# Attention scores from three half-height products, two heads at once on the row halves of TensorE, in place of two full-height products a head

## The chip, the cores and the metric

The kernel runs on one core of one Trainium2 chip. TensorE (PE) multiplies, VectorE (DVE), ScalarE (ACT) and GpSimd (POOL) work element by element, SyncE (SP) issues transfers. The metric is the device time of one execution in microseconds; of several runs the median counts.

## What is computed

Talking-heads attention over 4 batches of 12 heads with 448 positions of 64 channels, then a dense layer pair with a softmax-weighted activation:

```python
scores = scale * np.matmul(q, k.transpose(0, 1, 3, 2))
scores = np.einsum('bhij,hg->bgij', scores, w_pre)      # mix of the 12 heads
attn = softmax over j
attn = np.einsum('bhij,hg->bgij', attn, w_post)
x = np.matmul(attn, v)                                  # 1792 tokens x 768
h = x @ w_in;  solu = h * softmax(h);  layer norm * g_ln;  out = ln @ w_out
```

## The kernel before

Each float32 operand of the scores is split into two float16 parts, hi and lo, so that q times k is hi·hi + hi·lo + lo·hi. The tile `hl` holds, for every head, chunk and channel, hi and lo side by side: 2 x 64 channels make 128 columns, so a transpose of 112 x 128 puts hi on one half of the 128 rows and lo on the other. `turn_in` (L411) has SP issue these transposes as DMAs into `k1` and `q2`; for k of the first batch `turn_pe` (L427) transposes on PE and `turn_out` copies. In `q2` the halves lie the other way round than in `k1`, so that one product over 128 rows gives hi·lo + lo·hi. For hi·hi there is a second copy of q, `q1`, whose other half is zero: `clear_q1` (L455) sets the three tiles of it to zero once on POOL, and `move_hi` (L458) copies the hi half over by DMA after each transpose, one issue for a pair of heads, from ACT's queue in the first batch and from SP's afterwards.

`qk` (L473) makes the scores of one head and one block: two products of 448 columns, `q2` then `q1`, into one bank of `ps_s`, of which there are two. A batch is cut into four blocks of 88 or 120 rows (`ROWS`, L138). `score_hi` (L482) on ACT and `score_lo` (L488) on DVE empty the bank into the hi and lo part of the tile `s`; the bank is free after `score_lo`. In the first block of all, every other head uses a bank of `ps_o` (`spare`, L469).

Then the work goes in units of 10 rows, 45 in a batch. `fetch` (L506) has SP gather the rows of all 12 heads from `s` into `sr`, `premix` (L511) mixes heads with three products into `pm`, `rowmax`, `expo`, `guard`, `invert` and `weigh` (DVE, ACT, POOL) make the softmax, `postmix` (L557) mixes heads again (`po`), `post_out` empties it on ACT, and once a block is full `av` (L594) multiplies with v into `px`: 48 products that alternate between the two column halves of the array. `s` has two buffers, so the scores of a block are made while the block before it is consumed. After the last batch (from about 480 us) follow the dense layers, which the change does not touch.

The order of all instructions on all engines is made by the class `Plan` (L19): a list scheduler that simulates the engines with a cost in us for each task (`add`, L773 on), a due time, and rings (`ring`, `until`) for buffers: a task of ring `s` can only be placed when the holder two before it is done. Each engine executes its instructions in that order. `add_tasks` (L773) holds the tasks; those of the scores stand at L913 to L941, those of the transposes and the copy at L862 to L881.

Of the kernel before, what the change touches and what calls it, by code (L numbers as in the profile page):

```python
# [18 lines left out]
class Plan:  # L19
# [7 lines left out]
    def __init__(self, **rings):  # L27
        self.size = rings
        self.tasks = {}

    def add(self, key, run, on, after=(), behind=(), due=0.0, ring=None, until=(), lat=0.0):

        self.tasks[key] = (run, on, list(after), due, ring, list(until), lat, list(behind))

    def order(self):
# [10 lines left out]
        def ready(k, e):  # L46
# [5 lines left out]
            if ring and len(held[ring]) >= self.size[ring]:  # L52
                for a in held[ring][-self.size[ring]]:
# [6 lines left out]
        while len(out) < len(tasks):  # L60
# [27 lines left out]
            if ring:  # L88
                held[ring].append(until)
# [10 lines left out]
def kernel(  # L100
# [41 lines left out]
    QCH = 120  # L142
# [248 lines left out]
    def pair_views(n, b, p):  # L391
        x = raws[n, b][:, 2 * p : 2 * p + 2].rearrange("p h (c d) -> p (h c) d", c=NCH)
        y = hls[n, b][:, 2 * p : 2 * p + 2].rearrange("p h c s d -> p (h c) s d")
        i = (p + (n == "q")) % 2
        return x, y[:, :, i], y[:, :, 1 - i], scl[n, b][0][0:CP]

    def pair_hi(n, b, p, eng):
        if p == 0:
            hls[n, b] = hl_p.tile([CP, H, NCH, 2, D], F16, tag="hl", name=f"hl_{n}{b}")
# [3 lines left out]
    def pair_lo(n, b, p, eng):  # L403
# [4 lines left out]
        else:  # L408
            split_lo(lo, x, s, hi)

    def turn_in(n, b, p, m):  # L411
# [4 lines left out]
        if p == 0:  # L416
            x[b, g] = qk_p.tile([128, 2 * GP, S], F16, tag=f"{n}_{g}", name=f"{n}_{b}_{g}")
        h = 2 * GP * g + 2 * p
        nc.sync.dma_start_transpose(
            out=x[b, g][:, 2 * p : 2 * (p + m)].rearrange("p e (c i) -> p (e c) i", c=NCH),  # L420
            in_=hls[n, b][:, h : h + 2 * m].rearrange("p h c s d -> p (h c s d)"),
# [5 lines left out]
    def turn_pe(p):  # L427
        ps = tps[p] = ps_m.tile([128, 2, S], F16, tag="m", name=f"pt_{p}")
        for e in range(2):
            for c in range(NCH):  # L430
                nc.tensor.transpose(
                    out=ps[:, e, c * CP : (c + 1) * CP],
                    in_=hls["k", 0][:, 2 * p + e, c].rearrange("p s d -> p (s d)"),
# [3 lines left out]
    def turn_out(p, eng):  # L437
        g, i = divmod(p, GP)
        if i == 0:
            k1[0, g] = qk_p.tile([128, 2 * GP, S], F16, tag=f"k_{g}", name=f"k_0_{g}")  # L440
        copy(eng, k1[0, g][:, 2 * i : 2 * i + 2], tps.pop(p))
# [3 lines left out]
    def warm(e):  # L445
# [3 lines left out]
        x = hls["k", 0][:, 0, :, 0].rearrange("p c d -> p c d")  # L449
# [19 lines left out]
    def spare(b, c, h):  # L469

        return b == 0 and c == 0 and h % 2
# [34 lines left out]
    def fetch(b, u):  # L506
        c, r, step, _ = unit_rows(b, u)
        d = sr[b, u] = sr_p.tile([UK, 2, S], F16, tag="sr", name=f"sr_{b}_{u}")
# [896 lines left out]
```

## Time and profile before

| | us |
|---|---|
| median of 3 runs | 733.37 |
| lowest and highest run | 726.63, 737.01 |
| span of the profiled execution | 726.0 |
| PE busy, share of the span | 659.8, 91% |
| DVE, ACT, POOL busy | 495.6, 449.7, 275.4 |

The profile is of one execution; its span is that of the engines' instructions. Products are pipelined, so the durations shown for two products in a row overlap; the distance of their starts is what a product costs when PE is full. "Idle before" is the time in which an engine had nothing to run ahead of a group, with the work that ended it.

### The profile page before, as it was taken

To read this page: it belongs to the slowest core of one execution; us is meant where nothing else is said; L and a number is where in the kernel's file an instruction comes from. 1 tells how busy PE (TensorE), PEld (TensorE's weight loads), DVE (VectorE), ACT (ScalarE), POOL (GpSimd) and SP (SyncE) were. 2 spreads that over 40 slices of the span, in tenths; PEclk is the share of its full clock that TensorE was granted. 3 is DMA by queue.
4 is the path that set the end of the run, shared out by engine and by line. 5 is a ranking of instruction groups with operands and counts; after the bars stand their busy time and mean duration, and the time that the engine had idled before them with its cause. 6 is when DMAs were issued, how large, how long until landed. Compare 5 with 4: busy or idle time off the path is not lost.

```text
span 726.0 us, 14785 instructions
## 1 busy us (share of the span) xinstructions
PE 659.8 (91%) x5206; PEld 479.6 (66%) x5206; DVE 495.6 (68%) x1482; ACT 449.7 (62%) x956; POOL 275.4 (38%) x384
## 2 busy tenths in 40 slices
PE   3487998999997999999999989999998848999998
PEld 2346887888886878877888878774443424566664
DVE  6777996688985778996779999848888764200000
ACT  2567787787786787788788778744555544321111
POOL 6404781134851124771113353603667622320000
PEclk9789999999999999999999999999999989999999
DMA  8736497247577347677256645536456312243112
GB/s 228 121 90 199 136 221 212 84 135 228 180 198 200 87 105 213 199 209 212 95 180 204 212 153 188 139 98 187 121 121 151 68 20 51 51 103 95 44 44 65
DMA packets 121473, 102.47 MB, mean 141 GB/s; under 512 B 75524, under 2 KB 112056, under 8 KB 121400
## 3 DMA queue, kind: packets, MB, share of 16 engines
q1 hardware_dynamic: 115128, 87.07, 43.0%
q0 software_dynamic: 4384, 12.40, 6.4%
q10 hardware_dynamic: 1888, 2.07, 1.0%
q8 instruction: 41, 0.67, 0.4%
q14 instruction: 32, 0.26, 0.1%
HBM read 33.24 MB, written 9.63 MB: 59 GB/s over the span
## 4 chain that ended last, share of the span: by engine, by line
PE 61%; DVE 14%; DMA 11%; POOL 5%; ACT 3%; issue 2%; SPq 2%; DVEq 0%; POOLq 0%; ACTq 0%
PE po L561 15%; PE y L1314 14%; PE pm L515 12%; PE ps L480 9%; PE px L601 8%; DMA sr<-s 7%; PE ps_h L764 3%; DVE cv_wo L699 2%; POOL wo L702 2%; DVE cv_wo L694 1%; DMA raw_q<-in_q_dram 1%; DVE u L1257 1%; DVE wi L222 1%; DVE wo_l L222 1%; DMA q<-q 1%
## 5 line engine op out<-in xcount | busy, mean ns | idle before, releaser
L561 PEld LDWEIGHTS po<-wr,e 120*112 120x112 f32 x1440 | 173.5, 177 | 19.0 <-POOL wr L553 6.3
L561 PE MATMUL po<-wr,e 120*112 120x120 f32 x1440 | 178.6, 267 | 2.9 <-POOL wr L553 2.8
L553 POOL TENSOR_SCALAR wr<-wq,sm 120x120 f32<-120x120 f32 x180 | 78.0, 434 | 257.6 <-DVE sm L549 117.3
L532 ACT ACTIVATE e<-pm,nb,c_exp 120x448 f32<-120x448 f32 x180 | 131.4, 731 | 15.0 <-DVE e L520 9.5
L520 DVE TENSOR_SCALAR_CACHE_REDUCE e<-pm,c_nexp 120x448 f32<-120x448 f32 x180 | 121.2, 676 | 22.2 <-PE pm L515 12.5
L491 DVE SCALAR_TENSOR_TENSOR s<-ps,s 120x448 f16<-120x448 f32 (+1 forms) x192 | 116.9, 618 | 20.3 <-ACT s L486 17.9
L226 ACT COPY p_t<-po 112x480 f32<-112x480 f32 x180 | 104.0, 578 | 32.8 <-PE po L561 31.3
L486 ACT ACTIVATE s<-ps 120x448 f16<-120x448 f32 (+1 forms) x192 | 104.0, 548 | 28.1 <-PE ps L480 20.7
L515 PE MATMUL pm<-sr,wp_hi 120*120 120x448 f16 x360 | 100.5, 361 | 17.9 <-DMA sr<-s 16.8
L480 PE MATMUL ps<-k,q 128*120 128x448 f16 (+1 forms) x384 | 107.4, 366 | 7.8 <-DVE s L491 3.5
L764 PE MATMUL ps_h<-wi,xf 128*128 128x512 f16 x396 | 87.5, 379 | 3.7 <-DVE u L1257 3.6
L1314 PE MATMUL y<-wo_h,lth 128*128 128x384 f16 (+2 forms) x224 | 72.7, 331 | 9.9 <-ACT wo_h L217 9.9
L601 PE MATMUL px<-p_t,raw_v 112*64 112x120 f32 (+1 forms) x1536 | 80.7, 261 | 0.0
L601 PEld LDWEIGHTS px<-p_t,raw_v 112*64 112x64 f32 x1536 | 73.8, 137 | 8.7 <-issue 3.1
L1314 PE MATMUL y<-wo_l,lth 128*128 128x384 f16 (+2 forms) x224 | 72.7, 331 | 2.5 <-DVE wo_l L222 2.0
L1314 PEld LDWEIGHTS <-lth 128*128 128x128 f16 x448 | 44.3, 99 | 43.9 <-issue 15.3
L1314 PE MATMUL y<-wo_h,ltl 128*128 128x384 f16 (+2 forms) x224 | 72.8, 331 | 0.0
L764 PEld LDWEIGHTS <-xf 128*128 128x128 f16 x396 | 38.5, 98 | 49.2 <-issue 4.5
L515 PEld LDWEIGHTS <-wp_hi 120*120 120x120 f16 x360 | 43.2, 134 | 34.4 <-DMA sr<-s 19.9
L480 PEld LDWEIGHTS <-q 128*120 128x120 f16 (+1 forms) x384 | 47.8, 134 | 26.7 <-issue 10.4
L515 PE MATMUL pm<-sr,wp_lo 120*120 120x448 f16 x180 | 64.1, 356 | 0.0
L1322 ACT ACTIVATE o<-y,c_out 128x384 f32<-128x384 f32 (+2 forms) x28 | 16.1, 578 | 72.4 <-PE y L1314 72.4
(168 smaller groups left out, 820.6 us busy)
## 6 DMA issues: line engine op xcount, KB each, us to landing
sr<-s SPq DMA_DIRECT2D x180, 210.0 KB
cv_wi<-in_moe_w_in_dram SPq DMA_DIRECT2D x24, 256.0 KB
cv_wo<-in_moe_w_out_dram SPq DMA_DIRECT2D x8, 768.0 KB
raw_k<-in_k_dram POOLq DMA_DIRECT2D x18, 224.0 KB, 4.4
raw_q<-in_q_dram POOLq DMA_DIRECT2D x18, 224.0 KB, 4.2
raw_v<-in_v_dram POOLq DMA_DIRECT2D x18, 224.0 KB, 3.6
q<-q SPq DMA_DIRECT2D x18, 112.0 KB
xh<-xsh SPq DMA_DIRECT2D x9, 224.0 KB
```

The lines of the kernel that those rows point to most:

```text
L226: nc.scalar.copy(out=out, in_=in_)
L480: nc.tensor.matmul(y, x[:, e, i0 : i0 + n], k1[b, g][:, e], start=(a == 0), stop=(a == 1))
L486: nc.scalar.activation(out=s_t[b, c][0 : y.shape[0], h, 0], in_=y, func=AF.Copy, scale=2.0**-E_S)
L491: nc.vector.scalar_tensor_tensor(out=t[:, h, 1], in0=y, scalar=2.0**-E_S, in1=t[:, h, 0], op0=ALU.mult, op1=ALU.subtract)
L515: nc.tensor.matmul(ps[:, 0:S], w[0:UK], x[:, z], start=(a == 0), stop=(a == 2))
L520: nc.vector.tensor_scalar(out=e, in0=pmx[b, u][:, 0:S], scalar1=c_nexp[0:UK, b : b + 1], scalar2=None, op0=ALU.mult, op1=ALU.min, accum_ou ...
L532: nc.scalar.activation(out=ee[b, u], in_=pmx.pop((b, u))[:, 0:S], func=AF.Exp, bias=nbs.pop((b, u)), scale=c_exp[0:UK, b : b + 1], accum_o ...
L553: ENG[eng].tensor_scalar(out=w, in0=wq[0:UK, 0 : H * UN], scalar1=sums.pop((b, u)), scalar2=1.0, op0=ALU.mult, op1=ALU.mult)
L561: nc.tensor.matmul(ps[:, c * 120 : (c + 1) * 120], e[:, c * CP : (c + 1) * CP], w, start=True, stop=True)
L601: nc.tensor.matmul(xps[b, blk, g][e * 64 : e * 64 + 64, i, 0:n], raws["v", b][:, h, c * D : (c + 1) * D], block_view(b, blk, c * H + h), s ...
L764: nc.tensor.matmul(ps[:, n], xx[:, kc, o : o + 128], ww[:, kc, n * 512 : (n + 1) * 512], start=(kc == 0 and a == 0), stop=(kc == KDM - 1 a ...
L1314: nc.tensor.matmul(y, xx[:, kc], ww[:, kc, cut], start=(kc == 0 and a == 0), stop=(kc == KFF - 1 and a == 2),)
```

## The change

Hi and lo become separate products. `hl` is laid out by pairs of heads, so that a transpose puts one head on rows 0 to 63 and the other on rows 64 to 127, hi and lo in tiles of their own. A pair's scores are three steps (hi·hi, hi·lo, lo·hi), each with one product per head over its 64 rows, the two heads in turn, into two banks. `q1`, `clear_q1` and `move_hi` go. The products always take 128 rows of q (`QCH`), for which a block starts further up where it must, and `fetch` skips the rows that are too many. `Plan` learns that a task can hold several slots of a ring. `split_lo` of a pair is two instructions on DVE in place of one.

```diff
-    QCH = 120
+    QCH = 128
     def pair_views(n, b, p):
-        x = raws[n, b][:, 2 * p : 2 * p + 2].rearrange("p h (c d) -> p (h c) d", c=NCH)
-        y = hls[n, b][:, 2 * p : 2 * p + 2].rearrange("p h c s d -> p (h c) s d")
-        i = (p + (n == "q")) % 2
-        return x, y[:, :, i], y[:, :, 1 - i], scl[n, b][0][0:CP]
+        x = raws[n, b][:, 2 * p : 2 * p + 2].rearrange("p h (c d) -> p h c d", c=NCH)
+        hi, lo = (hls[n, b][:, p, s].rearrange("p c (h d) -> p h c d", h=2) for s in range(2))
+        return x, hi, lo, scl[n, b][0][0:CP]
...
-            split_lo(lo, x, s, hi)
+            for h in range(2):
+                split_lo(lo[:, h], x[:, h], s, hi[:, h])
...
-    q1 = [qk_p.tile([128, 2 * GP, S], F16, tag=f"q1_{g}", name=f"q1_{g}") for g in range(NPAIR // GP)]
-    def clear_q1(g):
-        nc.gpsimd.memset(q1[g], 0.0)
-    def move_hi(b, p, m):
-        for j in range(p, p + m):
-            g, i = divmod(j, GP)
-            lo, e = 64 * i, slice(2 * i, 2 * i + 2)
-            eng = nc.sync if b else nc.scalar
-            eng.dma_start(out=q1[g][lo : lo + 64, e], in_=q2[b, g][64 - lo : 128 - lo, e])
...
-    def qk(b, c, h):
-        i0, n = ROW0[b][c], ROWS[b][c]
-        pool, tag = (ps_o, "o") if spare(b, c, h) else (ps_s, "s")
-        ps = pool.tile([128, 512], F32, tag=tag, name=f"ps_{b}_{c}_{h}")
-        y = sps[b, c, h] = ps[0:n, 0:S]
-        g, e = divmod(h, 2 * GP)
-        for a, x in enumerate((q2[b, g], q1[g])):
-            nc.tensor.matmul(y, x[:, e, i0 : i0 + n], k1[b, g][:, e], start=(a == 0), stop=(a == 1))
+    def qk_rows(b, c):
+        i0 = min(ROW0[b][c], S - QCH)
+        return i0, ROW0[b][c] - i0
+    def qk(b, c, p):
+        i0, _ = qk_rows(b, c)
+        pool, tag = (ps_o, "o") if spare(b, c, p) else (ps_s, "s")
+        for e in range(2):
+            ps = pool.tile([128, 512], F32, tag=tag, name=f"ps_{b}_{c}_{2 * p + e}")
+            sps[b, c, 2 * p + e] = ps[:, 0:S]
+        g, j = divmod(p, GP)
+        for a, (x, z) in enumerate(((0, 0), (0, 1), (1, 0))):
+            for e in range(2):
+                w = slice(64 * e, 64 * e + 64)
+                nc.tensor.matmul(
+                    sps[b, c, 2 * p + e],
+                    q2[b, g][w, j, x, i0 : i0 + QCH],
+                    k1[b, g][w, j, z],
+                    start=(a == 0),
+                    stop=(a == 2),
+                )
...
-                    add(
-                        ("qk", b, c, h),
-                        one(qk, b, c, h),
-                        {"pe": 0.38},
-                        after=before + [("t", "k", b, ...), ("q1", b, ...)],
-                        due=due,
-                        ring="o" if spare(b, c, h) else "s",
-                        until=[("sl", b, c, h)],
-                    )
+                    if h % 2 == 0:
+                        add(
+                            ("qk", b, c, p),
+                            one(qk, b, c, p),
+                            {"pe": 0.66},
+                            after=before + [("t", "k", b, ...), ("t", "q", b, ...)],
+                            due=due,
+                            ring="o" if spare(b, c, p) else "s",
+                            until=[[("sl", b, c, h + e)] for e in range(2)],
+                            slots=2,
+                        )
```

## Rows read from the trace of the kernel before

**Rows 1.** The page: busy time, share of the span and instructions of each engine.
```profile
PE 659.8 (91%) x5206; PEld 479.6 (66%) x5206; DVE 495.6 (68%) x1482; ACT 449.7 (62%) x956; POOL 275.4 (38%) x384
```

**Rows 2.** Stretches: length, busy time by engine, granted clock, DMA share, GB/s.
```profile
24.00:60.00 36.00, 24.04 (x107) 14.48 (x107) 26.21 (x66) 22.90 (x49) 8.73 (x14) 0.76 0.66 141
60.00:120.00 60.00, 55.03 (x518) 46.61 (x518) 49.03 (x165) 45.60 (x107) 35.45 (x58) 1.00 0.71 191
...
420.00:480.00 60.00, 56.04 (x517) 46.15 (x516) 53.73 (x156) 46.03 (x101) 27.98 (x34) 1.00 0.47 145
```

**Rows 3.** PE's groups, 60 to 480 us: busy, mean ns, idle before and its enders.
```profile
L515 PE MATMUL pm<-sr,wp_hi 120*120 120x448 f16 x346 | 95.8, 358 | 17.1 <-DMA sr<-s 16.0 <-ACT e L532 0.7
L480 PE MATMUL ps<-k,q 128*120 128x448 f16 x262 | 71.3, 354 | 2.4 <-DVE s L491 1.3 <-DVE p_v L166 0.8 <-ACT e L532 0.2
```

**Rows 4.** PE's timeline, 203.8 to 205.1 us: start, length (ends overlap), instruction, count.
```profile
203.83 0.54 PE L480 MATMUL ps<-k,q 128*88 128x448 f16 x2
204.21 0.98 PE L561 MATMUL po<-wr,e 120*112 120x120 f32 x8
205.03 0.54 PE L515 MATMUL pm<-sr,wp_hi 120*120 120x448 f16 x2
```

**Rows 5.** PE's timeline around a visit of `px` with 120 columns.
```profile
185.53 0.35 PE L515 MATMUL pm<-sr,wp_lo 120*120 120x448 f16 x1
185.81 2.68 PE L601 MATMUL px<-p_t,raw_v 112*64 112x120 f32 x48
188.42 0.59 PE L480 MATMUL ps<-k,q 128*120 128x448 f16 x2
188.85 0.38 PE L189 MATMUL spread_q<-ident,amx_q 128*128 128x128 f32 x2
```

**Rows 6.** PE's timeline around a visit of `px` with 88 columns.
```profile
73.94 2.04 PE L601 MATMUL px<-p_t,raw_v 112*64 112x88 f32 x48
75.91 0.59 PE L480 MATMUL ps<-k,q 128*120 128x448 f16 x2
```

**Rows 7.** The chain that ended last, at the start: start, length, work.
```profile
25.77 4.08 DMA q<-hl_q
29.93 6.37 DMA q<-q
...
42.78 3.85 DMA sr<-s
...
58.74 7.71 DMA sr<-s
```

**Rows 8.** The timeline of all engines at the start, in brackets idle time before.
```profile
23.00 8.61 SPq L419 DMA_TRANSPOSE q<-hl_q  x6
...
46.57 0.62 DVE L491 SCALAR_TENSOR_TENSOR s<-ps,s 120x448 f16<-120x448 f32 x1 [0.67 <-ACT s L486]
```

**Rows 9.** The timeline at the third change of batch.
```profile
227.41 2.04 SPq L464 DMA_DIRECT2D q<-q  x2
...
231.24 1.78 SPq L509 DMA_DIRECT2D sr<-s  x2
...
234.11 0.88 PE L515 MATMUL pm<-sr,wp_hi 120*120 120x448 f16 x2 [3.76 <-DMA sr<-s]
```

**Rows 10.** The line of the copy: ns min/median/max of an issue, first and last.
```profile
L464 SPq DMA_DIRECT2D q<-q x18: 518/566/1456, 102.8 to 342.4; - x18
```

**Rows 11.** One head from its products to its freed bank, on the timeline.
```profile
248.03 0.54 PE L480 MATMUL ps<-k,q 128*88 128x448 f16 x2
...
248.74 0.62 ACT L486 ACTIVATE s<-ps 88x448 f16<-88x448 f32 x1
...
249.39 0.62 DVE L491 SCALAR_TENSOR_TENSOR s<-ps,s 88x448 f16<-88x448 f32 x1 [0.27 <-ACT s L486]
```

**Rows 12.** The line of `split_lo`, 0 to 480 us: ns min/median/max of one.
```profile
L222 DVE SCALAR_TENSOR_TENSOR xsl<-px,x_sc,xsh x96: 226/332/343, 80.7 to 477.7; 128x120 f16<-128x120 f32 x72, 128x80 f16<-128x80 f32 x18, 128x24 f16<-128x24 f32 x6
L222 DVE SCALAR_TENSOR_TENSOR hl_q<-raw_q,p_q,hl_q x20: 729/742/1166, 22.1 to 321.6; 112x512 f16<-112x512 f32 x20
```

More of the change, by code (lines that the diff above doesn't have):

```diff
@@ L29, in __init__, with add @@
         self.tasks = {}
-    def add(self, key, run, on, after=(), behind=(), due=0.0, ring=None, until=(), lat=0.0):
+        self.slots = {}
+    def add(self, key, run, on, after=(), behind=(), due=0.0, ring=None, until=(), lat=0.0, slots=None):
+        if slots:
+            self.slots[key] = slots
         self.tasks[key] = (run, on, list(after), due, ring, list(until), lat, list(behind))
@@ L51, in ready @@
                 r = max(r, end + lat + (0.06 if eng == e else self.WAIT))
-            if ring and len(held[ring]) >= self.size[ring]:
-                for a in held[ring][-self.size[ring]]:
+            for i in range(self.slots.get(k, 1) if ring else 0):
+                n = len(held[ring]) + i - self.size[ring]
+                for a in held[ring][n] if n >= 0 else ():
                     if a not in done:
@@ L88, in order @@
             if ring:
-                held[ring].append(until)
+                held[ring].extend(until if k in self.slots else [until])
             avail.remove(k)
@@ L416, in turn_in @@
         if p == 0:
-            x[b, g] = qk_p.tile([128, 2 * GP, S], F16, tag=f"{n}_{g}", name=f"{n}_{b}_{g}")
-        h = 2 * GP * g + 2 * p
+            x[b, g] = qk_p.tile([128, GP, 2, S], F16, tag=f"{n}_{g}", name=f"{n}_{b}_{g}")
+        j = GP * g + p
         nc.sync.dma_start_transpose(
-            out=x[b, g][:, 2 * p : 2 * (p + m)].rearrange("p e (c i) -> p (e c) i", c=NCH),
-            in_=hls[n, b][:, h : h + 2 * m].rearrange("p h c s d -> p (h c s d)"),
+            out=x[b, g][:, p : p + m].rearrange("p a s (c i) -> p (a s c) i", c=NCH),
+            in_=hls[n, b][:, j : j + m].rearrange("p a s c x -> p (a s c x)"),
         )
@@ L428, in turn_pe @@
         ps = tps[p] = ps_m.tile([128, 2, S], F16, tag="m", name=f"pt_{p}")
-        for e in range(2):
+        for s in range(2):
             for c in range(NCH):
                 nc.tensor.transpose(
-                    out=ps[:, e, c * CP : (c + 1) * CP],
-                    in_=hls["k", 0][:, 2 * p + e, c].rearrange("p s d -> p (s d)"),
+                    out=ps[:, s, c * CP : (c + 1) * CP],
+                    in_=hls["k", 0][:, p, s, c],
                     identity=ident[0:CP, 0:CP],
@@ L439, in turn_out @@
         if i == 0:
-            k1[0, g] = qk_p.tile([128, 2 * GP, S], F16, tag=f"k_{g}", name=f"k_0_{g}")
-        copy(eng, k1[0, g][:, 2 * i : 2 * i + 2], tps.pop(p))
+            k1[0, g] = qk_p.tile([128, GP, 2, S], F16, tag=f"k_{g}", name=f"k_0_{g}")
+        copy(eng, k1[0, g][:, i], tps.pop(p))
     warm_ps = []
@@ L507, in fetch @@
         c, r, step, _ = unit_rows(b, u)
+        r += qk_rows(b, c)[1]
         d = sr[b, u] = sr_p.tile([UK, 2, S], F16, tag="sr", name=f"sr_{b}_{u}")
@@ L795, in add_tasks @@
             last = ("mix", i)
-        for g in range(NPAIR // GP):
-            add(("cl", g), one(clear_q1, g), {"pool": 1.6}, due=3.0 + g)
         turns = ([(p, GP) for p in range(0, NPAIR, GP)], [(0, 1), (1, 1), (2, 1), (3, 1), (4, 1), (5, 1)])
@@ L868, in add_tasks @@
                         after=[("lo", n, b, j) for j in range(p, p + m)]
-                        + ([] if z else [("qk", b - 1, NQ - 1, h) for h in range(2 * p, 2 * (p + m), 2)]),
+                        + ([] if z else [("qk", b - 1, NQ - 1, j) for j in range(p, p + m)]),
                         due=due,
@@ L872, in add_tasks @@
                     )
-                    if n == "q":
-                        add(
-                            ("q1", b, p),
-                            one(move_hi, b, p, m),
-                            {"act": 0.1 * m} if z else {"sp": 0.6 * m},
-                            after=[("t", n, b, p)] + [("cl", g) for g in range(NPAIR // GP)],
-                            due=due + 1.5,
-                            lat=2.6,
-                        )
             add(("es", b), one(exp_scales, b), {"dve": 0.15}, after=es, due=at(b - 1, 35) if b else T0 - -2)
@@ L917, in add_tasks @@
                     due = at(b, u0 - 6) - STEP * 0.6 * (H - h)
[L918 to L931 removed]
+                    p = h // 2
+                    if h % 2 == 0:
[3 more added lines that the diff above has]
+                            {"pe": 0.66},
+                            after=before
+                            + [
+                                ("t", "k", b, p if z else p // GP * GP),
+                                ("t", "q", b, max(j for j, _ in turns[z] if j <= p)),
+                            ],
+                            due=due,
[3 more added lines that the diff above has]
+                        )
+                        before = [("qk", b, c, p)]
                     add(
@@ L935, in add_tasks @@
                         {"act": 0.43},
-                        after=[("qk", b, c, h)] + ([("sh", b, c, h - 1)] if h else []),
+                        after=[("qk", b, c, p)] + ([("sh", b, c, h - 1)] if h else []),
                         due=due + 0.4,
```

16 lines of the change are left out of this document (4 added, 12 removed).

## The prediction
> **What bounds the kernel now.** I read the page first: of the profiled span TensorE (PE) is busy 91%, far ahead of the other engines [rows 1]. A share over the whole span mixes stages, so next comes the table of stretches [rows 2]. The reader is to see two regimes. From 24 to 60 us PE works 24.0 of 36 us at a granted clock of 0.76: it starves. From 60 to 480 us (seven stretches of 60; the first and the last stand there) it works 55 to 58 of 60 us at full clock, so here PE's own time sets the pace. The groups of PE in that stretch say what ends its idle time: premixes that wait for the transfer of `sr` (16 us in 420); ahead of the scores it idles 2.4 us in all [rows 3]. Whatever this change saves or adds on PE between 60 and 480 us should therefore show almost undiminished in the span; after 480 us the change touches nothing. The same rows give the pace: 346 premix products with `wp_hi`, two per unit, are 173 units in 420 us, 2.43 us each, so a block of 12 units lasts 29 us.
>
> The chain of waits gives the third thing: at the start it runs through the copy `q<-q` (6.4 us) and then twice through `sr` transfers [rows 7].
>
> **The change part by part.**
>
> *Products.* Now a head costs two products of 448 columns, the next product starting 0.38 us after the first: 203.83 to 204.21 [rows 4]. Two heads are 0.76 us. After the change a pair costs three steps, each a product per head on its own half of the rows. If the two halves stream abreast, the stream is 3 x 0.19 = 0.57 us. There are 16 blocks x 6 pairs = 96 pairs, so abreast and free of any other cost this gives 96 x 0.19 = 18.2 us.
>
> No row shows row halves. The nearest are the `px` products, which use the two column halves in alternation (64 columns each). They do run abreast: 48 of them, 24 pairs, take 2.61 us at 120 columns and 1.97 us at 88 [rows 5, 6], which is 0.054 us each at 120, where the same kind of product on the whole array needs 0.82 / 8 = 0.10 us (`po`, 204.21 to 205.03) [rows 4]. But the visit has a fixed cost. The difference of the two sizes is 0.64 us for 32 columns, 0.02 us a column, so 120 columns are 2.40 us and 0.21 us is left over, of which a few ns for each of the 24 pairs (some 0.06 us) recur and 0.15 us is paid once. Ahead of it, the first `px` starts 0.28 us after the last `pm`, where 0.19 us is the rule: 0.09 more. After it the two `ps` products take 0.43 us (188.42 to 188.85) where 0.38 is the rule: 0.05 more [rows 4, 5]. So going to halves and back costs 0.09 + 0.15 + 0.05 = 0.29 us a visit.
>
> That 0.29 us, if row halves pay it too, decides the case. The `px` visits carry 48 products each; a score pair carries six, stands alone between products of the whole array, and can't be joined to the next pair, because the pair holds both banks of `ps_s`. Its cost is then 0.57 + 0.29 = 0.86 us against 0.76: 96 x 0.10 = +9.6 us. The bounds are 0.57 us (nothing, -18.2 us) and 0.86 us (as the column halves, +9.6 us). I take 0.86, the only row there is. Halfway, 0.66 to 0.72 us, is open too: the planner's entry in the diff for the pair is 0.66, which orders the work and is no measurement.
>
> The Trainium skill speaks to this in TensorEngine Tiling, Key Properties: a change of tiling mode, not merely of tile, drains the engine, and two row tiles of 64 are a mode of their own. By it each pair drains twice, as the trace shows for column halves; no row here shows it for row halves. Without the rule the sum for PE would be -18.2 us, with it +9.6 us.
>
> *Weights.* Six loads of 64 rows x 128 columns replace four of 128 x 120 or 128 x 88. Loads lie under the products ahead of them (the products are evenly 0.19 us apart), except at the switch, which the 0.29 us holds already.
>
> *The copy `q<-q`.* Removed: 6 issues on ACT at the start, 18 on SP at a median of 0.57 us [rows 10], and the clearing of `q1` on POOL. At the start the scores no longer wait for the copy but for the transposes alone. SP issues six of these from 23.00 to 31.6 us, 1.4 us apart [rows 8]; on the chain one takes 4.1 us from issue to the copy that follows it [rows 7], so the last lands at about 34 to 35. Three steps at half clock (1.1 us), one `score_hi` (0.62 [rows 11]) and two `score_lo` (1.24 [rows 8]) after it put the end of the first block at 38, where now its first `sr` goes out at 42.78 [rows 7]: up to -5 us. Not all of it stays. The next block must be done before the stall at 58.74, where `sr` takes 7.71 us to arrive [rows 7], and its pairs go one at a time (below): six holds of 3 us from 38 are 56, which leaves -2 to -3. I take -4.
>
> At the three changes of batch the copies stand in SP's queue between transposes and `sr`: at 227.41 two of them occupy SP for 2.04 us, a transpose follows, `sr` goes out at 231.24, and PE stands for 3.76 us [rows 9]. Without them the fetch leaves some 2 us earlier. The other two places show smaller stalls. I take -3 us, between 0 (SP is late for another reason) and -5.
>
> *Residuals.* A `lo` on DVE becomes two instructions of 256 elements. A `lo` of 512 takes 0.74 us, an `xsl` of 120 at most 0.34 [rows 12]: two pieces cost at most 0.25 us more each, there are 20 for q and no more than that for k, so at most 10 us, spread over 450. DVE is busy 49 to 54 of 60 us [rows 2] and covers it; without cover those 10 us would be added. Taken: 0. The transposes keep their number and size, and the `hi` pieces write the same 512 elements in another order. The scores' rows grow from 120 or 88 to 128, which should lengthen nothing: 88 and 120 rows cost the same 0.62 us on DVE [rows 8, 11].
>
> *Banks.* Now a head holds one of two banks from its product to the end of its `score_lo`: 248.03 to 250.01, 2.0 us [rows 11]. After, a pair holds both: 0.86 + 0.2 until ACT starts, 2 x 0.62 on ACT, 0.1 and 0.62 on DVE, 3.0 us, and the next pair begins only then. Six of them are 18 us of the block's 29. Queued behind a pair that waits are premix and postmix on PE's in-order queue. While the planner finds other PE work for the time, it costs nothing; taken: 0.
>
> *Sum.* +9.6 - 4 - 3 = +2.6 us. On the profiled span of 726.0 that is 728.6; this span stands 7.4 us under the median of the three runs (733.4, from 726.6 to 737.0), so on the median 736.
>
> **The rivals.**
> 1. *The row halves switch for less.* At 0.66 us a pair PE gains 9.6 us: -9.6 - 7 = -16.6, 717 us. For it: a pair's second half could load while the first streams, as `px` loads do. Against: `px` pays in full each time.
> 2. *They switch for nothing.* -18.2 - 7 = -25.2, 708 us. The Trainium skill, TensorE: Matmul & The Clock Gate, Part 2, has weight loads pulled ahead of running products where row groups don't conflict; by that the loads at a switch would hide. The `px` load that opens a visit wasn't hidden here.
> 3. *The banks become the wait (the other side).* With ACT's and DVE's work of the units in between, a hold can grow from 3.0 to over 4.8 us, six of which are a block's 29 us; from there on PE waits at the pair, and `sr` is late behind it. Already now the second block's `sr` leaves only when its scores end (58.74). If a third of the 90 pairs behind the first block make PE wait 0.5 us, that is 15 us more than the forecast: 751 us. Against: PE idles only 2.4 us before `ps` now, with DVE named [rows 3].
> 4. *The halves don't run abreast.* 6 x 0.19 + 0.29 = 1.43 us a pair, +64 us: 793 us. The `px` rows speak against it.
>
> **How the numbers follow.** My forecast 0.45 (736), rival 1 0.22 (717), rival 2 0.17 (708), rival 3 0.12 (751), rival 4 0.04 (793). The terms for start and SP are uncertain by 5 us either way, and so is each case. The range from 712 to 752 leaves out most of rival 2 (0.11), rival 4 and a part of rival 3 (0.04): 0.19. The forecast's own range is 729 to 745. Over 2% is about what a measurement can tell from no change, that is below 718.7 or above 748.0. Faster: nearly all of rival 2, over half of rival 1: 0.30. Slower: rival 4, over half of rival 3, a little of the forecast: 0.15. Within 2%: 0.55.
>
> **What would show it.** On PE: the two products of a step within 0.01 us of each other (rival 4 if 0.19); from a pair's first product to the next work 0.86 us less the 0.09 ahead of it (rivals 1 and 2: 0.57 to 0.66), and the 0.28 us step ahead of it. At the start: first `sr` issue at 38 us, no `q<-q`. At the third change of batch: `sr` issues directly behind the transposes, and a stall of PE near 2 us in place of 3.76. PE's idle time before `ps`, with DVE named: 2 to 5 us; 15 and more is rival 3. What would make the prediction wrong: a switch cost for rows unlike that for columns, above all, then a re-planned order that moves the 20 us of PE's stalls in either direction.

## The result and the profile after

| | before | after |
|---|---|---|
| median, us (12 runs each, same chip) | 731.17 (726.63 to 737.01) | 737.25 (734.39 to 739.23) |
| ratio, 95% interval | | 1.0089 (1.0064 to 1.0114) |
| span of the profiled execution, us | 726.0 | 736.9 |

The change costs 6 us, 0.9%: measurable with this many runs, and within 2%. The forecast was 736 from a base of 733. The number fits, and most of its terms don't.

The page after: span, then busy time by engine as in [rows 1].

```profile
span 736.9 us, 15167 instructions
PE 672.2 (91%) x5398; PEld 451.7 (61%) x5398; DVE 503.8 (68%) x1515; ACT 449.4 (61%) x954; POOL 269.2 (37%) x383
```

The stretches after, columns as in [rows 2], with one of 6 us added.

```profile
24.00:60.00 36.00, 26.30 (x128) 11.76 (x130) 26.43 (x71) 20.97 (x47) 10.16 (x16) 0.71 0.58 141
60.00:66.00 6.00, 6.00 (x39) 4.18 (x37) 2.98 (x9) 3.64 (x9) 0.36 (x1) 0.73 0.04 14
...
420.00:480.00 60.00, 56.45 (x534) 45.15 (x535) 55.64 (x156) 45.41 (x100) 29.93 (x33) 1.00 0.49 153
```

PE's groups after, 60 to 480 us, as in [rows 3].

```profile
L520 PE MATMUL pm<-sr,wp_hi 120*120 120x448 f16 x344 | 96.8, 363 | 13.0 <-DMA sr<-s 9.0 <-ACT e L537 3.4 <-DVE amx_v L203 0.3
...
L478 PE MATMUL ps<-k,q 64*128 64x448 f16 x510 | 65.2, 355 | 1.2 <-DVE sm L551 0.6 <-DVE s L495 0.5
```

The steady middle is hardly changed: PE is as busy as before, waits less for `sr` (9.0 us against 16.0) and no more ahead of `ps`. So the loss is elsewhere. To place it, I cut each span at starts on PE that any reader can find in the timeline: the first premix of all, the first premix of the second block, the last premix, and the first product `y` of the dense layers. The table gives the length of each part, rounded so that a line adds up to its span. "Second block" runs from the first premix of all to that of the second block, the time in which the second block's scores are finished; "seam" is the stretch from the last premix to `y`. The run e4 is the kernel before, profiled once more, so the first two lines show how far two executions of one program differ. A span lies some 2 us under the time of its run, and the run that was profiled isn't always a typical one: that of e2 took 3.3 us more than the median of its runs, that of e3 4.2, that of e11 11.0.

| profiled execution | to first premix | second block | other blocks | seam to `y` | dense | span |
|---|---|---|---|---|---|---|
| before | 46.8 | 19.7 | 408.4 | 112.0 | 139.1 | 726.0 |
| e4, before again | 47.4 | 19.4 | 411.6 | 112.0 | 138.5 | 728.9 |
| **after** | **41.8** | **27.7** | **407.0** | **121.4** | **139.0** | **736.9** |
| e1, four full products | 42.5 | 29.0 | 406.9 | 119.7 | 140.0 | 738.1 |
| e2, three full products | 43.7 | 27.4 | 400.2 | 121.4 | 139.0 | 731.8 |
| e3, before without copies | 42.0 | 19.2 | 414.7 | 112.0 | 138.9 | 726.8 |
| e5, after, planner's cost 0.70 | 41.0 | 27.9 | 408.3 | 113.9 | 139.0 | 730.1 |
| e6, full products head by head | 44.6 | 19.6 | 402.8 | 119.7 | 138.8 | 725.4 |
| e7, before with pairs | 47.2 | 27.1 | 409.6 | 111.3 | 139.0 | 734.1 |
| e8, copies on DVE and ACT | 43.4 | 19.5 | 417.9 | 112.0 | 139.1 | 731.8 |
| e9, first copies on DVE | 44.8 | 19.2 | 414.1 | 111.9 | 137.8 | 727.9 |
| e10, after with three banks | 43.0 | 20.1 | 427.7 | 111.7 | 137.4 | 739.9 |
| e11, as e6 on half the rows | 46.5 | 25.1 | 444.9 | 119.9 | 137.4 | 773.9 |
| e12, after, planner's cost 0.57 | 41.7 | 21.4 | 405.3 | 120.4 | 138.6 | 727.4 |

Against the two profiles of before, the change brings -5.0 to -5.6 us at the start, costs 8.0 to 8.3 in the second block, brings -1.4 to -4.6 in the blocks behind it, and costs 9.4 in the seam, which the prediction said the change doesn't touch.

**The second block.** Timeline of PE after, 53 to 70 us (start, length, instruction, count, in brackets the idle time before).

```profile
53.52 0.74 PE L478 MATMUL ps<-k,q 64*128 64x448 f16 x6
...
56.15 0.74 PE L520 MATMUL pm<-sr,wp_hi 120*120 120x448 f16 x2 [1.88 <-DMA sr<-s]
...
58.59 1.00 PE L520 MATMUL pm<-sr,wp_hi 120*120 120x448 f16 x2 [1.33 <-DMA sr<-s]
...
59.90 1.30 PE L478 MATMUL ps<-k,q 64*128 64x448 f16 x6
...
69.53 0.54 PE L520 MATMUL pm<-sr,wp_hi 120*120 120x448 f16 x2
```

The other engines there: the last `score_lo` of the block and the `sr` behind it.

```profile
64.41 0.62 DVE L495 SCALAR_TENSOR_TENSOR s<-ps,s 128x448 f16<-128x448 f32 x1
...
65.06 2.50 SPq L514 DMA_DIRECT2D sr<-s  x3
```

Before, at the same place:

```profile
57.98 0.62 DVE L491 SCALAR_TENSOR_TENSOR s<-ps,s 120x448 f16<-120x448 f32 x1
...
66.50 0.59 PE L515 MATMUL pm<-sr,wp_hi 120*120 120x448 f16 x2 [0.70 <-DMA sr<-s]
```

The block's six pairs start at 36.87, 38.90, 44.66, 48.80, 53.52 and 59.90. The last one stands in PE's in-order queue behind two premixes of the first block which wait for `sr`, 1.88 and 1.33 us. It then runs at the lower of the clock's two levels (a pair takes 1.30 in place of 0.74; the granted clock of 60 to 66 us is 0.73, after PE had worked 26 of the 36 us before). Its last `score_lo` ends at 65.0, and `sr` leaves 0.03 us later. Not all of this is PE's queue: the other head's `score_lo` ends at 62.4, and the last one stands in DVE's order behind a step of softmax that starts at 63.80, after 1.14 us of waiting for `po`. Before, the scores ended at 58.6 although they began later.

**The seam.** Timeline of PE and POOL after, around the last premix (476.48) and the first `y`.

```profile
472.64 5.24 POOL L223 TENSOR_SCALAR wi<-wi,p_wi 128x1024 f16<-128x1024 f32 x3
476.48 0.54 PE L520 MATMUL pm<-sr,wp_hi 120*120 120x448 f16 x2
477.86 1.33 POOL L558 TENSOR_SCALAR wr<-wq,sm 120x120 f32<-120x120 f32 x1
479.16 3.17 POOL L223 TENSOR_SCALAR wi<-wi,p_wi 128x1024 f16<-128x1024 f32 x2
...
485.35 1.07 PE L566 MATMUL po<-wr,e 120*112 120x120 f32 x8 [2.44 <-POOL wr L558]
...
597.91 0.80 PE L1309 MATMUL y<-wo_h,lth 128*128 128x384 f16 x2 [6.32 <-ACT wo_h L221]
```

Before, at the same place:

```profile
467.76 3.17 POOL L219 TENSOR_SCALAR wi<-wi,p_wi 128x1024 f16<-128x1024 f32 x2
474.91 0.54 PE L515 MATMUL pm<-sr,wp_hi 120*120 120x448 f16 x2
...
586.88 0.80 PE L1314 MATMUL y<-wo_h,lth 128*128 128x384 f16 x2 [6.32 <-ACT wo_h L217]
```

Nothing in the diff speaks of these instructions. The planner, given other costs and slots ahead of them, put the preparation of the dense weights `wi` on POOL around the last premix, ahead of the attention's last weights `wr`: it ends at 482.3, 5.9 us after the start of that premix. Before, it ended at 470.9, 4.0 us ahead of it. From last premix to first `y` it is 121.4 us against 112.0. The chain of work that ended last, after, runs through these pieces and through `wi`'s next step on DVE (start, length, work):

```profile
475.29 2.59 POOL wi L223 x2
...
479.19 2.06 POOL wi L223
...
481.27 2.13 DVE wi L226
```

The two go together in all fourteen profiles of the table: where the last `wi` on POOL ends ahead of the last premix (by 4.0 to 6.6 us), the seam is 111.3 to 113.9; where it ends behind it (by 3.1 to 5.9 us), 119.7 to 121.4. The last `po` ends 15.0 us after the last premix starts, before 6.6; that is most of the 9.4.

**The pair.** PE's timeline after, one pair between `po` and `pm`, as in [rows 4].

```profile
153.39 0.98 PE L566 MATMUL po<-wr,e 120*112 120x120 f32 x8
154.31 0.74 PE L478 MATMUL ps<-k,q 64*128 64x448 f16 x6
154.98 0.59 PE L520 MATMUL pm<-sr,wp_hi 120*120 120x448 f16 x2
155.41 0.35 PE L520 MATMUL pm<-sr,wp_lo 120*120 120x448 f16 x1
```

Eight `po` take 0.82 us [rows 4], so the pair could start at 154.21 and starts 0.10 late. To `pm` it is 0.67 us, and the two `pm` products behind it take 0.43 where 0.38 is the rule. Sum: 0.10 + 0.67 + 0.05 = 0.82 us, against 0.86 forecast and 0.76 for two heads before. With a stream of 0.57, going to row halves and back costs 0.25 us. The first product of each half starts 3 ns after the other in the trace.

One pair is not all of them. Over the 51 pairs that stand between `po` or `pm` at full clock, with no wait at either end, the medians are 0.82 us with `pm` behind and 0.86 with `po` behind (the eight `po` then take 0.91). And 22 of the 96 pairs stand directly behind a visit of `px`, where nothing is paid ahead:

```profile
140.88 2.68 PE L606 MATMUL px<-p_t,raw_v 112*64 112x120 f32 x48
143.49 0.74 PE L478 MATMUL ps<-k,q 64*128 64x448 f16 x6
144.16 1.07 PE L566 MATMUL po<-wr,e 120*112 120x120 f32 x8
145.07 0.54 PE L520 MATMUL pm<-sr,wp_hi 120*120 120x448 f16 x2
```

The 48 `px` take 2.61 us, as they do between products of the whole array [rows 5], and the pair 0.67. In e1 below, whose pairs use the whole array, a pair behind `px` takes 0.77, so these 22 cost no more than full products do. Added up over the 96 pairs, the halves cost PE some 4 us by this, an estimate.

### The profile page after: what moved, and what is told of

Same layout as the page of the kernel before. It is cut to its first block, busy times and chain, and to the rows that moved or that the text cites. A ratio compares the mean times of both kernels' runs of the same rounds, so it can differ in the third digit from the quotient of the medians.

```text
span 736.9 us, 15167 instructions
## 1 busy us (share of the span) xinstructions
PE 672.2 (91%) x5398; PEld 451.7 (61%) x5398; DVE 503.8 (68%) x1515; ACT 449.4 (61%) x954; POOL 269.2 (37%) x383
## 4 chain that ended last, share of the span: by engine, by line
PE 51%; DVE 13%; DMA 10%; POOL 5%; ACT 2%; issue 2%; SPq 0%; POOLq 0%; ACTq 0%; DVEq 0%
PE y L1309 14%; PE po L566 12%; PE pm L520 9%; PE px L606 8%; DMA sr<-s 8%; PE ps L478 5%; PE ps_h L769 3%; POOL wo L707 2%; DVE cv_wo L704 2%; DVE cv_wo L699 1%; DVE u L1252 1%; DVE s L495 1%; DVE wo_l L226 1%; DMA raw_k<-in_k_dram 1%; DVE e L525 1%
## 5 line engine op out<-in xcount | busy, mean ns | idle before, releaser
L566 PEld LDWEIGHTS po<-wr,e 120*112 120x112 f32 x1440 | 169.9, 179 | 32.2 <-POOL wr L558 13.3
L566 PE MATMUL po<-wr,e 120*112 120x120 f32 x1440 | 181.7, 271 | 5.9 <-POOL wr L558 5.2
L558 POOL TENSOR_SCALAR wr<-wq,sm 120x120 f32<-120x120 f32 x180 | 74.8, 417 | 266.0 <-DVE sm L554 158.3
L495 DVE SCALAR_TENSOR_TENSOR s<-ps,s 128x448 f16<-128x448 f32 x192 | 114.5, 618 | 13.9 <-ACT s L490 12.8
L520 PE MATMUL pm<-sr,wp_hi 120*120 120x448 f16 x360 | 102.8, 368 | 18.7 <-DMA sr<-s 14.7
L490 ACT ACTIVATE s<-ps 128x448 f16<-128x448 f32 x192 | 98.8, 546 | 22.8 <-PE ps L478 16.2
L478 PE MATMUL ps<-k,q 64*128 64x448 f16 x576 | 78.6, 371 | 6.1 <-DMA q<-hl_q 3.9
L1309 PEld LDWEIGHTS <-lth 128*128 128x128 f16 x448 | 44.7, 100 | 43.7 <-issue 15.7
L520 PEld LDWEIGHTS <-wp_hi 120*120 120x120 f16 x360 | 39.3, 133 | 47.1 <-issue 24.9
L1317 ACT ACTIVATE o<-y,c_out 128x384 f32<-128x384 f32 (+2 forms) x28 | 16.1, 577 | 72.4 <-PE y L1309 72.4
L478 PEld LDWEIGHTS <-q 64*128 64x128 f16 x576 | 22.5, 96 | 39.3 <-issue 18.8
```

The lines of the kernel that those rows point to most:

```text
L478: nc.tensor.matmul(sps[b, c, 2 * p + e], q2[b, g][w, j, x, i0 : i0 + QCH], k1[b, g][w, j, z], start=(a == 0), stop=(a == 2),)
L490: nc.scalar.activation(out=s_t[b, c][0 : y.shape[0], h, 0], in_=y, func=AF.Copy, scale=2.0**-E_S)
L495: nc.vector.scalar_tensor_tensor(out=t[:, h, 1], in0=y, scalar=2.0**-E_S, in1=t[:, h, 0], op0=ALU.mult, op1=ALU.subtract)
L520: nc.tensor.matmul(ps[:, 0:S], w[0:UK], x[:, z], start=(a == 0), stop=(a == 2))
L558: ENG[eng].tensor_scalar(out=w, in0=wq[0:UK, 0 : H * UN], scalar1=sums.pop((b, u)), scalar2=1.0, op0=ALU.mult, op1=ALU.mult)
L566: nc.tensor.matmul(ps[:, c * 120 : (c + 1) * 120], e[:, c * CP : (c + 1) * CP], w, start=True, stop=True)
```

## The experiments

First batch: what the row halves, the saved products and the copies are worth.

**e1_full4**: the change with its products undone, two over the full height for each head.

```diff
-        for a, (x, z) in enumerate(((0, 0), (0, 1), (1, 0))):
+        for a in range(2):
             for e in range(2):
-                    q2[b, g][w, j, x, i0 : i0 + QCH], k1[b, g][w, j, z],
+                    q2[b, g][:, j, a, i0 : i0 + QCH], k1[b, g][:, j, a],
```

> The changed kernel, order of all engines unchanged, with a pair's scores from four products over all 128 rows instead of six over 64 (the products mix two heads, so the scores aren't those of the reference; only the array's mode and the number of products change). Theory A (the switch to row halves and back is what the pair pays): in the changed kernel a pair takes 0.096 us ahead, 0.39 + 0.28 us from its first product to the next work and 0.05 us behind, 0.815 us; here 4 x 0.19 = 0.76 us, so -0.055 us x 96 = -5 us: 732 us. Rival B (the re-planned order and the pair's two banks set the time, not the product's mode): 737 us, within 1.5. In the trace the step ahead of a pair falls from 0.28 to 0.19 us by either theory.

Measured: 739.19 us, 1.0109 (1.0070 to 1.0148) of before, where after was 1.0089. Without any row halves the kernel is as slow. In the table e1 and after agree in every part within 1.7 us. So the halves neither gain nor lose anything that shows, and the whole loss belongs to what came with them: pairs as one task, and the new order.

**e2_full3**: three full-height products for a pair, a quarter of e1's left out.

```diff
-        for a in range(2):
-            for e in range(2):
+        for a, e in ((0, 0), (0, 1), (1, 0)):
```

> The changed kernel with a pair's scores from only three products over 128 rows (0.57 us, one head has one product fewer and the heads are mixed, so the scores aren't the reference's): what the row halves would cost if a switch were free. Theory A, PE's own time sets the pace from 60 to 480 us: -0.245 us x 96 = -23 us against the changed kernel, 714 us. Rival B, order and banks set the time: between 727 and 737 us.

Measured: 730.19 us, 1.0002 (0.9973 to 1.0030). A product less in every pair is 96 x 0.19 = 18 us, with neighbours undisturbed; the time falls by 9.0. Between first and last premix, the distances of PE's starts (waits over 60 ns taken out) sum to 55.2 us for `ps` against 70.9 in e1, 15.7 less; those waits sum to 31.9 against 23.8, 8.1 more. Half of what PE is spared returns as waiting, so the rule "PE's own time sets the pace" holds by half here.

**e3_no_copy**: the kernel before, `move_hi` without effect.

```diff
     def move_hi(b, p, m):
-        for j in range(p, p + m): ...
+        return
```

> The kernel before, its order unchanged, with the 24 copies of q's hi half not issued (q1 stays zero, so hi times hi is missing from the scores). The prediction's two terms for the copy: -4 us at the start and -3 us at the changes of batch, 724 us against 731. Rival: the start's gain is given back before unit 9, because the second block's scores decide there; then no more than -3 us, 728 or above.

Measured: 724.30 us, 0.9882 (0.9845 to 0.9920). The prediction's -4 and -3 for the copies are confirmed in sum. In its profile the start is 4.8 to 5.4 us shorter and the second block keeps that: its first premix runs at 61.23, before at 66.50. The later part can't be read from it: this run took 4.2 us more than the median, and its middle is longer than before's by 3 to 6 us, so the profile shows the gain at the start and not the gain of the whole. PE's idle time ahead of premixes with `sr` named is 16.1 us in it, as before. That it is 9.0 after then comes with the new order rather than with the absence of the copies, as far as one profile tells.

**e4_before_again** is the kernel before, for one more profile.

> The kernel before, unchanged, for a second profile: the first profile was of an execution some 5 us faster than the median. Expected: 731 us, and the stretch from the last premix to the first output product (112 us in the first profile) longer by some of these 5 us, if that is where executions differ; otherwise the stretch from the first to the last premix (428 us).

Measured: one run of 730.65 us, span 728.9. The seam is 112.0 again; the middle differs by 3 us.

Second batch: the seam, the pairs, and the copies on another engine.

**e5_cost70**: the change with another number in the planner; every instruction is there as after, in another order.

```diff
-                            {"pe": 0.66},
+                            {"pe": 0.70},
```

> The changed kernel with one number different: the planner's cost of a score pair is 0.70 us in place of 0.66, so the same work runs in another order. Theory C (some 9 us of the loss are the order around the end of attention, where the preparation of w_in comes late and its pieces stand on POOL and DVE ahead of the last units' work): the stretch from the last premix to the first output product, 121 us in the changed kernel and 112 before, falls back to 111 to 114, and the time to 728 to 730 us. Rival A (the row halves' switch is the loss): nothing changes, 737 us.

Measured: 731.69 us, 1.0008 (0.9982 to 1.0034), 5.6 us under after. Last premix and first `y` in its timeline:

```profile
477.23 0.54 PE L520 MATMUL pm<-sr,wp_hi 120*120 120x448 f16 x2
...
591.15 0.80 PE L1309 MATMUL y<-wo_h,lth 128*128 128x384 f16 x2 [5.77 <-ACT wo_h L221]
```

The last premix comes as late as after, `y` 6.8 us earlier: the seam is 113.9. So its length here is a matter of order alone. The last piece of `wi` stands on POOL here:

```profile
470.10 1.12 POOL L223 TENSOR_SCALAR wi<-wi,p_wi 128x1024 f16<-128x1024 f32 x1
```

It ends at 471.2, 6.0 us ahead of the last premix, as before it does by 4.0. That the place of `wi` is what lengthens the seam fits the chain of waits and all fourteen profiles; moving `wi` alone wasn't tried.

**e6_single**: e1 with each head a task of its own, as before the change.

```diff
-    def qk(b, c, p):   # a pair, two slots, {"pe": 0.66}
+    def qk(b, c, h):   # a head, one slot, {"pe": 0.38}
```

> e1_full4 with the pairing taken back: two products over 128 rows for each head as a task of its own, one bank each, the changed kernel's layout and no copy of q (heads mixed, so the scores aren't the reference's). The same products as e1_full4, other tasks and so another order. Theory B (a pair holds both banks, so a block's scores end late, and sr leaves the moment they end): slack of 4 us and more returns between the end of a block's scores and its sr, and the time falls from 739 to 724 to 728 us. Rival (pairing costs nothing, the order's scatter does): 733 to 740.

Measured: 727.13 us, 0.9924 (0.9890 to 0.9958), 12 us under e1 for the same products. In the profiles 9.4 of this lie in the second block. Its scores end at 56.1, and its first premix runs at

```profile
64.17 0.59 PE L513 MATMUL pm<-sr,wp_hi 120*120 120x448 f16 x2 [1.16 <-DMA sr<-s]
```

**e7_before_pairs**: the reverse, the kernel before with two heads as one task.

```diff
-    def qk(b, c, h):   # a head, one slot, {"pe": 0.38}
+    def qk(b, c, p):   # both heads' products in turn, two slots, {"pe": 0.76}
```

> The kernel before with one part of the change alone: scores of two heads as one task that holds both banks, with the same four full-height products and the copies of q as before. Theory B: the pairing alone makes it slower, 738 to 742 us against 730. Rival (pairing costs nothing): 728 to 733.

Measured: 738.35 us, 1.0106 (1.0061 to 1.0152). Nothing else is changed but the order that follows from it, and the kernel before loses 8 us, as much as the whole change. The place is the same:

```profile
69.44 0.62 DVE L499 SCALAR_TENSOR_TENSOR s<-ps,s 120x448 f16<-120x448 f32 x1 [1.39 <-ACT s L494]
...
74.31 0.54 PE L523 MATMUL pm<-sr,wp_hi 120*120 120x448 f16 x2
```

The second block is 27.1 us against 19.7; the other blocks and the seam (409.6, 111.3) are those of before.

**e8_engine_copy**: the kernel before, its copies on DVE or ACT in place of DMA.

```diff
-            eng.dma_start(out=q1[g][lo : lo + 64, e], in_=q2[b, g][64 - lo : 128 - lo, e])
+            copy(eng, q1[g][lo : lo + 64, e], q2[b, g][64 - lo : 128 - lo, e])
```

> The kernel before with q's hi half moved by a copy on DVE or ACT (64 rows shifted by 64) in place of the DMA, heads one at a time and products as before: all results are those of the reference. If the copy's waits are worth what e3_no_copy showed, 5 to 8 us, and DVE and ACT cover 24 copies of 0.3 to 0.9 us: 723 to 726 us. Rival (the copies on busy engines cost what they save): 730.

Measured: 732.69 us, 1.0054 (1.0018 to 1.0090). First premix at 43.4 and that of the second block at 62.9, 3.6 us earlier than before, then 417.9 us for the other blocks against 408 to 412. The start's gain is given back.

Third batch: the banks, the price of the switch where it is large, another order.

**e9_first_copy**: e8 for the first batch only, on DVE; DMA afterwards.

```diff
+            if b:
+                nc.sync.dma_start(out=q1[g][lo : lo + 64, e], in_=q2[b, g][64 - lo : 128 - lo, e])
+            else:
+                copy(eng, q1[g][lo : lo + 64, e], q2[b, g][64 - lo : 128 - lo, e])
```

> The kernel before with q's hi half copied by DVE in the first batch only, and by DMA from SP in the other three, as before; all results are those of the reference. If e8_engine_copy lost its gain to the 18 copies on busy engines between 60 and 480 us, the start's 4 us stay and nothing else is lost: 726 to 728 us against 730.5. Rival (the new order scatters by as much as the start gives): 729 to 734.

Measured: 730.22 us, 0.9991 (0.9961 to 1.0022): no difference. The 2.5 us gained by the second block's premix (64.0) are gone at the end of the middle.

**e10_three_banks**: after with three banks for scores, taken from premix.

```diff
-    ps_s: bufs=2    ps_m: bufs=3    Plan(s=2, m=3)
+    ps_s: bufs=3    ps_m: bufs=2    Plan(s=3, m=2)
```

> The changed kernel with three banks for scores in place of two, taken from the premix (two in place of three), so that a pair's first half can start while one bank of the pair before is still held. Theory B: the second block's scores end some 5 us sooner, its first premix falls from 69.5 to about 64 us, and blocks whose sr leaves the moment the scores end get fewer than 6 of 14; what the premix loses with two banks isn't known, so for the whole 730 to 742 us. Rival (pairing isn't what makes the second block late): first premix of the second block at 69 us or later.

Measured: 739.99 us, 1.0118 (1.0075 to 1.0161). The second block is back to 20.1 us:

```profile
63.12 0.54 PE L520 MATMUL pm<-sr,wp_hi 120*120 120x448 f16 x2 [0.22 <-ACT e L537]
```

So that stretch is relieved by a third bank, as the theory of the banks wants it. The price is paid in the other blocks, 427.7 us against 407.0, which eats that and the shorter seam (111.7). That premix with two banks is its cause fits PE's idle time ahead of premix (60 to 480 us: 21.3 us, 6.3 of them with ACT's `e` named, against 13.0 and 3.4 after); the granted clock of that stretch is 0.98 in place of 1.00, and the two weren't taken apart.

**e11_half_single**: e6 on 64 of the 128 rows, so that every head visits a row half alone, 192 visits.

```diff
-                sps[b, c, h], q2[b, g][:, j, x, i0 : i0 + QCH], k1[b, g][:, j, x], ...
+                sps[b, c, h], q2[b, g][0:64, j, x, i0 : i0 + QCH], k1[b, g][0:64, j, x], ...
```

> e6_single, order unchanged, with each head's two products over the 64 lower rows only (the other 64 rows are left out, so the scores aren't the reference's): the same streams, with a switch to row halves and back for each of 192 heads. By the changed kernel's trace a switch and back is 0.096 + 0.09 + 0.05 = 0.236 us, 45 us in all. Theory A, in its place here (so much more than PE's idle time can't hide): 727 + 30 to 45 = 757 to 772 us. Rival (a switch is hidden, as 5 us of it were between e1_full4 and the changed kernel): under 740.

Measured: 764.66 us, 1.0459 (1.0408 to 1.0511), 37.5 us more than e6 with the same number and length of products. A visit on PE's timeline:

```profile
181.44 0.98 PE L559 MATMUL po<-wr,e 120*112 120x120 f32 x8
182.35 0.55 PE L475 MATMUL ps<-k,q 64*128 64x448 f16 x2
182.83 0.59 PE L513 MATMUL pm<-sr,wp_hi 120*120 120x448 f16 x2
183.26 0.35 PE L513 MATMUL pm<-sr,wp_lo 120*120 120x448 f16 x1
```

0.09 ahead (0.91 for eight `po` in place of 0.82), 0.48 where 0.38 is the rule, 0.43 where 0.38 is: 0.24 us a visit, and 0.28 with `po` behind (medians of the visits at full clock); at 0.24 it is 46 us in 192. Here no halves run abreast to pay for the switch. The 37.5 us in the time aren't the switch alone, though: in the profiles the granted clock of 60 to 480 us is 0.97, in e6 1.00, and over whole runs, without the longest, it is 0.964 to 0.971, in e6 0.973 to 0.988. By the difference of the means, 0.015, up to 11 of the 37.5 us can be the clock, an estimate.

**e12_cost57**: as e5, with the pair's bare stream as its cost.

```diff
-                            {"pe": 0.66},
+                            {"pe": 0.57},
```

> The changed kernel with the planner's cost of a pair at 0.57 us in place of 0.66: the same work in a third order. Theory C (the order at the end of attention is worth 7 to 9 us, and the rest of the loss is pairing): between 728 and 734 us, with the stretch from the last premix to the first output product at 111 to 114 us if it is under 732. Rival: 737, whatever the order.

Measured: 727.35 us, 0.9955 (0.9923 to 0.9986). The same instructions as after, 10 us faster, and a little faster than before: the one version of the change that beats it. The gain isn't where it was expected, in the seam, but in the second block. Where after's last pair of the second block ran at 59.90, here it runs at 55.40:

```profile
55.40 0.74 PE L478 MATMUL ps<-k,q 64*128 64x448 f16 x6
...
57.50 1.15 DVE L495 SCALAR_TENSOR_TENSOR s<-ps,s 128x448 f16<-128x448 f32 x2
...
63.09 0.54 PE L520 MATMUL pm<-sr,wp_hi 120*120 120x448 f16 x2
```

The pairs hold both banks as after, and the block takes 21.4 us in place of 27.7. Pairs don't cost those 8 us by themselves, then: they leave the planner six places in the block in place of twelve, and of the orders with pairs and two banks, those at a cost of 0.66, 0.70 and, in e7, 0.76 put the last one late, that at 0.57 doesn't. The seam is still 120.4: the last `wi` ends at 471.6, 3.1 us after the start of the last premix (468.45).

## Why the prediction was right, and where not

The time came within 1 us of the forecast, and that is luck: the median moved by +6.1 us where +2.6 was forecast, the base of 733.4 from three runs is 731.2 from twelve, and the terms behind the +2.6 are others than those measured. By steps:

1. **The pair's price: right in kind, half in size.** The halves stream abreast, and the switch to rows is paid both ways: 0.82 to 0.86 us against 0.86 forecast, where products of the whole array stand on both sides; behind `px` it is less, so that +9.6 us over all pairs is some +4. Rival 4 (halves one after the other; its own sum gives 791, not 793) is out, and rival 2 too, since the switch isn't free. Rival 1's sign did appear: from a pair's first product to the next work it is 0.67 us, near its 0.66 and under the 0.77 that was to speak for the forecast, because the visit itself holds 0.10 of fixed cost and not 0.15. But the 0.66 was to be all that a pair costs, and 0.10 ahead and 0.05 to 0.09 behind come on top. This agrees with the Trainium skill, TensorEngine Tiling (Array Packing), Key Properties, which has a change of tiling mode drain TensorE; the trace gives the price that the page doesn't, 0.24 to 0.29 us there and back.
2. **From price to time: wrong.** The step "whatever this change saves or adds on PE should show almost undiminished" made +9.6 us of it, and would make +4 of the measured price. Between e1 and after, which differ in this alone, medians and parts agree within 2 us, and after is if anything the faster. The distances of PE's starts between first and last premix (as for e2) sum to 412.1 us in e1 and 413.2 after: `ps` 8.2 less, `pm` 4.3 and `po` 5.0 more behind and ahead of the visits. Waits shrink by 2.3 and cover these 1.1; where the rest of the 4 us went wasn't taken apart. e2 shows the same from the other side: half of what PE is spared becomes waiting. In e11, where 46 us and more are added, most of it shows. So small terms on PE can vanish in the waits for `sr`, which are 16 us before, and a large one comes through.
3. **The start, -4: right in size, given back at once.** First `sr` at 37.77 (forecast 38), no `q<-q`, first premix 5 us earlier:

```profile
37.77 2.69 SPq L514 DMA_DIRECT2D sr<-s  x3
```

   The step that failed is "six holds of 3 us from 38 are 56". The hold was near (3.0 forecast, 3.3 us from 154.31 to 157.62 further on), but pairs don't follow each other at their holds: each waits for its place in PE's queue, behind premixes that wait for `sr`. From 36.87 to 59.90 they stand 4.6 us apart on average, and the scores end at 65.0. The prediction had this place in view (the stall at 58.74): its holds would have left -2 to -3 of the start's -5, it took -4, and the second block gave back 8.
4. **SP at the changes of batch, -3: not shown.** The stall at the third change is nearly gone after, with the transposes and `sr` one behind the other and PE idle 0.41 us, for ACT, where it was 3.76 for `sr` [rows 9]:

```profile
231.07 1.40 SPq L423 DMA_TRANSPOSE k<-hl_k  x1
232.91 0.81 SPq L514 DMA_DIRECT2D sr<-s  x1
233.77 1.51 SPq L423 DMA_TRANSPOSE q<-hl_q  x1
```

   But e3, which has no copies and the old order, keeps 16.1 us of waits for `sr` in the middle of its profile, and at this place PE waits twice, 1.62 and 1.65 us, although `sr` leaves directly behind the transposes, at 228.78. The copies' worth in all (5.5 us by e3's medians, 5.8 to 11.3 by its interval) is confirmed; of the parts its profile shows the start's 5 us and no other.
5. **Banks, 0: wrong.** This is rival 3, right in direction and wrong in what was to be looked for. It was to show as idle time of PE ahead of `ps` with DVE named, 15 us and more; PE idles 1.2 us there in all, 0.5 of them for `score_lo`, against 2.4 and 1.3 before [rows 3]. The price appears one step later, as a late `sr` in one block, 8 us. e6 and e10 take it away by undoing the pairs or adding a bank, e7 brings it into the kernel before, e12 removes it by order.
6. **After 480 us nothing: wrong.** The new order cost 9.4 us there. The prediction named a re-planned order only as something that moves PE's stalls; in a kernel whose order is computed, a changed cost reaches work that the diff doesn't touch.

The residual on DVE, taken at 0, has the size that was estimated: a `lo` piece of 256 takes 0.48 us, two where one took 0.74, and DVE is busy 503.8 us against 495.6. No run takes it away by itself, so that it costs nothing isn't shown.

Together: -5, +8, -1 to -5 and +9.4 in place of -4, -3 and +9.6. They add up to 7 to 11 us, more than the medians' 6.1, because the profiled run after was slower than the median of its runs and those of before were faster. The forecast's sum fits because an overlooked cost of order stands where a cost of the array was put.

What stays open: how much of the second block's loss is pairs and how much order, since every run that changes the one re-plans the other. Three orders of the same instructions measured 737.25, 731.69 and 727.35, a spread larger than the result, so the result is that of one order. An order with e12's blocks and the seam of before (112.0) would be some 8 us under e12, about 719; it wasn't run, and what places `wi` wasn't taken apart.

## What to carry to other kernels

A switch between the whole array and its row halves has to be earned within one visit: 0.25 to 0.29 us, more than the 0.19 that a pair saves here, so either many products share a visit, or it stands directly behind another visit to a part of the array (as the pairs behind `px` do), or it doesn't pay. Joining two tasks into one that holds all buffers of a ring halves the places at which a scheduler can put them; look for the block in which the joined task stands behind something that waits. And where a program orders the instructions, measure a change in several orders (another planner's cost will do) before its few microseconds are read as its own.

## What the runs showed of the hardware

Weight loads of 64 rows and 128 columns take 96 ns where those of 120 columns take 133, although 120 is less. The rows aren't the reason: in e1, loads of 128 rows and 128 columns take 98 ns (before, those of 88 columns take 120). After:

```profile
L520 PEld LDWEIGHTS <-wp_hi 120*120 120x120 f16 x360 | 39.3, 133 | 47.1 <-issue 24.9
...
L478 PEld LDWEIGHTS <-q 64*128 64x128 f16 x576 | 22.5, 96 | 39.3 <-issue 18.8
```

And the load at a switch isn't hidden. The loads of the pair shown above and of the `pm` behind it, on PE's timeline of weight loads:

```profile
154.30 0.30 PEld L478 LDWEIGHTS <-q 64*128 64x128 f16 x6
154.98 0.18 PEld L520 LDWEIGHTS <-wp_hi 120*120 120x120 f16 x2 [0.37 <-issue]
155.22 0.13 PEld L520 LDWEIGHTS <-wp_lo 120*120 120x120 f16 x1
```

Within `pm` the load of `wp_lo` begins 0.19 us ahead of its product (155.22, 155.41), under the product before. At both ends of the pair the first load is shown at the very start of its product (154.30 and 154.31, 154.98 and 154.98), and that product comes late. The Trainium skill, TensorE: Matmul & The Clock Gate, Part 2, has loads pulled ahead where row groups don't conflict or the background buffer is the target; in these traces that holds between products of one mode and not across the change of mode.
